# The second layer of a fused attention and feed-forward kernel, transposed and split twice

## The chip, the cores and the metric

The kernel runs on one core of a Trainium2 chip. The metric is device time in microseconds for one execution, from the first to the last instruction with what the device adds around it. Three runs of the kernel before took 933.7, 934.85 and 936.31 us; the median is 934.85. A profile of one more execution shows what each engine did: TensorE multiplies matrices (PE, with its weight loads as PEld), VectorE (DVE), ScalarE (ACT) and GpSimd (POOL) work elementwise, and SyncE (SP) issues DMAs.

## The reference

Four batches of 768 tokens pass through attention with 8 heads of 64 columns, where a query sees only the keys that fall into the same of 16 clusters. The result `x`, 3072 tokens by 512, goes through two matrix products:

```python
def _moe_ref(x, w_in, w_out):            # x 3072x512, w_in 512x2048, w_out 2048x512
    h = x @ w_in
    g = h * (1.0 / (1.0 + np.exp(-1.702 * h)))
    return (g @ w_out).astype(np.float32)
```

Inputs and output are 32-bit floats, except that the weights arrive as 64-bit and are rounded in the kernel.

## The kernel before

Everything is written in the order in which each engine is to run it; no scheduler moves instructions. An engine runs its own list in order, and waits where an operand of another engine isn't there yet or a buffer isn't free. All loads and stores stand in one list, that of SP.

**Attention** takes about the first 350 us. A loop over `t` works on pairs of heads; `scores`, `part`, `exps`, `values`, `row_sums_of` and `normalise` make the transposed result X of one pair and one half of the tokens, a tile of 128 x 384. The weights are rounded beside it (`rounding`), a chunk at a time. X of batches 0 to 2 stays in SBUF (pool `xp`); X of batch 3 is stored to a DRAM tile `kept` (L561) and read back after the first layer of batch 0 (L843).

**The first layer** uses a block method: a product of 2 x 2 blocks is made from seven block products in place of eight, with sums of blocks ahead of and after them. For batch `b`, `first7(b, f, X, T)` makes, for `f` in 0 to 7, blocks `f` and `f + 8` of the 16 blocks of `G`, for both halves of the tokens. Each product has two matmuls (L744, weights stationary, 384 columns of X moving). `sums_w` (POOL, L589) makes the sums of w_in two steps ahead, `sums_x` (DVE) those of X for the next batch. `add` (L735) takes results out of PSUM. `gelu` is a tanh on ScalarE (L579) and a product on DVE (L580).

**The second layer** uses the same method once. `second7(b, n, sg)` works on tokens `n*128` to `n*128+127` of both halves, three times a batch. Here the activations in `G` are stationary and 256 columns of w_out (or of its sums, `Z`) move: seven products of eight matmuls (L801). `sums_g(n)` makes the sums of G on DVE ahead of each `n`, `sums_z` those of w_out on POOL in batch 0. The results lie with tokens on the partitions, so a store is one plain DMA (L807).

A 32-bit matmul is two instructions in the profile: seven products of eight matmuls, three times, are 336 instructions a batch; the first layer has 8 x 7 x 2 x 2 = 224.

**PSUM.** `ps_b` has six banks that both layers use in turn; a bank is free when the last copy or addition has read it.

The last instruction but for the closing of the program is the store of the last block (L807); a test whether the fast path was valid (`okt`, `bad`) ends the program.

Of the kernel before, what the change touches and what calls it, by code (L numbers as in the profile page):

```python
# [8 lines left out]
FP32 = mybir.dt.float32  # L9
# [4 lines left out]
AF = mybir.ActivationFunctionType  # L14
# [24 lines left out]
def fast(  # L39
# [40 lines left out]
    LIMIT = float(2 ** 20)  # L80
    FAR = float(2 ** 120)
    CODE = float(2 ** 50)
    NX = 6 * HP
    SQ = 32
    assert D == 64 and NC == 16 and H * NC == P and NJ == 6 and DM == H * D

# [422 lines left out]
    def values(u):  # L509
        g, kt = divmod(u, NJ)  # L510
        p, h = split(g)
        if kt == 0:
            o_of[g] = ps_o.tile([P, 2, 512], FP32, name="o")
        A = A_of.pop(u)
        for r in range(2):
            rows = slice(r * D, (r + 1) * D)
            for a in range(2):
                nc.tensor.matmul(out=o_of[g][a * D:(a + 1) * D, r, 0:HALF],  # L518
                                 lhsT=v_in[p][rows, a, kt, :],
                                 rhs=A[rows, a, :],  # L520
                                 start=(kt == 0), stop=(kt == NJ - 1))
        if kt == NJ - 1:
            o = o_of.pop(g)
            O_of[g] = (xp if p < NPAIR - HP else xl).tile(
                [P, HALF], FP32, name="x"), short()
            for r in range(2):
                nc.scalar.copy(O_of[g][r], o[:, r, 0:HALF])
# [13 lines left out]
    def normalise(g):  # L541
# [13 lines left out]
        x, more = O_of.pop(g)  # L555
        nc.vector.tensor_tensor(out=x, in0=x, in1=more, op=ALU.add)  # L556
        nc.vector.tensor_tensor(out=x, in0=x, in1=rec, op=ALU.mult)
        if b < B - 1:
            xT_of[b, h, hp] = x
        else:  # L560
            nc.sync.dma_start(out=kept[h, hp], in_=x)  # L561

    recs = {}
    kept = spill.tile([2, HP, P, HALF], FP32, name="kept")

    def check(g):

# [5 lines left out]
                             scale=-2.0 * LIMIT * LIMIT,  # L573
                             accum_out=row_sums[:, 1, g:g + 1])


    def gelu(g, t, h):

        nc.scalar.activation(out=t, in_=h, func=AF.Tanh, scale=1.702)  # L579
        nc.vector.scalar_tensor_tensor(out=g, in0=t, scalar=1.0, in1=h,  # L580
                                       op0=ALU.add, op1=ALU.mult)

    def out_rows(b, h, n):
        return out[b * S:(b + 1) * S, :].rearrange(
            "(j p) n -> p j n", p=P)[:, h * NH + n, :]

    def sums(engine, todo):
        for o, a, op, b in todo:
            engine.tensor_tensor(out=o, in0=a, in1=b, op=(  # L589
                ALU.add if op == "+" else ALU.subtract))  # L590
# [10 lines left out]
    def sums_w(i):  # L601
# [8 lines left out]
        if i < FB:  # L610
# [1 line left out]
        sums(nc.gpsimd, ((S[2], A22, "-", S[3]), (S[1], S[2], "+", A11),  # L612
                         (S[4], A12, "-", S[2])))

    T_of.update({(i, c): tp.tile([P, HALF], FP32, name=f"T{i}{c}")
                 for i in (2, 3, 4) for c in range(2)})

    def sums_x(b):

        X = {(r, h, c): xT_of.pop((b, h, 2 * r + c))  # L620
             for r in range(2) for h in range(2) for c in range(2)}
        T = {(i, c): T_of[i, c] for i in (2, 3, 4) for c in range(2)}
        for c in range(2):
            T[1, c] = X[0, 1, c]
        for o, a, z in ((3, (1, 1), 1), (1, 1, (0, 0)), (2, (1, 1), 1),
# [32 lines left out]
    for t in range(NT + 2):  # L658
# [28 lines left out]
        while work and PREP[work[0][1]] == prep_near:  # L687
            prep(*work.pop(0))
        if t >= NT - 8 and t < NT:
            XT = next(made)  # L690
        for p, i in work:
            prep(p, i)
        for _ in range(0 if t in (0, 1, 2, NT - 1) else 5 if t == 4 else
# [14 lines left out]

    gp = ctx.enter_context(tc.tile_pool(name="gp", bufs=NF // 4))
    yp = ctx.enter_context(tc.tile_pool(name="yp", bufs=1))
    sp = ctx.enter_context(tc.tile_pool(name="sp", bufs=1))
    th = ctx.enter_context(tc.tile_pool(name="th", bufs=1))
    ps_b = ctx.enter_context(tc.tile_pool(name="ps_b", bufs=6, space=PS))
    G = sp.tile([P, NF, 2, HALF], FP32, name="G")
    Z_of = {i: sp.tile([P, FB, DN], FP32, name=f"Z{i}") for i in (2, 3, 4)}
    S4 = [sp.tile([P, 4, P], FP32, name=f"S{q}") for q in range(2)]
    y2 = sp.tile([P, DM], FP32, name="y2")

    def Bz(row, col, f):

        return w_out[:, row * FB + f, col * DN:(col + 1) * DN]

    def Tz(i, f):
        return Bz(0, 1, f) if i == 1 else Z_of[i][:, f]

    def sums_z(f):
        sums(nc.gpsimd, ((Tz(3, f), Bz(1, 1, f), "-", Bz(0, 1, f)),
                         (Tz(1, f), Bz(0, 1, f), "-", Bz(0, 0, f)),  # L730
                         (Tz(2, f), Bz(1, 1, f), "-", Tz(1, f)),
                         (Tz(4, f), Bz(1, 0, f), "-", Tz(2, f))))

    def add(o, p, a):
        nc.vector.tensor_tensor(out=o, in0=p, in1=a, op=ALU.add)  # L735
# [1 line left out]
    def first7(b, f, X, T):  # L737
# [8 lines left out]
            return ps[:, 0:HALF]  # L746

        def finish(g):
            gelu(g, th.tile([P, HALF], FP32, name="th"), g)

        g1, g2 = G[:, f], G[:, f + FB]
        p = product(A_in(0, 0, f), lambda c: X[0, 0, c])
# [16 lines left out]
        finish(g2[:, 0])  # L769
        finish(g1[:, 0])  # L770

    def A_out(h, m, q, n):

        at = m * FB + 4 * q
        return G[:, at:at + 4, h, n * P:(n + 1) * P]

    def sums_g(n):

        S = {}
        for q in range(2):  # L780
            for i in (1, 2, 4):
                S[i, q] = (gp.tile([P, 4, P], FP32, name="g") if i < 4 else
                           S4[q])
            S[3, q] = A_out(1, 0, q, n)
            sums(nc.vector, (
                (S[1, q], S[3, q], "+", A_out(1, 1, q, n)),
                (S[2, q], S[1, q], "-", A_out(0, 0, q, n)),
                (S[4, q], A_out(0, 1, q, n), "-", S[2, q]),
                (S[3, q], A_out(0, 0, q, n), "-", S[3, q])))
        return S  # L790

    def second7(b, n, sg):

        ys = [yp.tile([P, DM], FP32, name="y"), y2]
        C = {10 * (h + 1) + m + 1: ys[h][:, m * DN:(m + 1) * DN]
             for h in range(2) for m in range(2)}

        def product(a, z):
            ps = ps_b.tile([P, 512], FP32, name="b")
            for f in range(FB):  # L800
                nc.tensor.matmul(out=ps[:, 0:DN], lhsT=a(f // 4)[:, f % 4],  # L801
                                 rhs=z(f), start=(f == 0), stop=(f == FB - 1))
            return ps[:, 0:DN]

        def store(h, m=None):
            cols = slice(0, DM) if m is None else slice(m * DN, (m + 1) * DN)
            nc.sync.dma_start(out=out_rows(b, h, n)[:, cols],  # L807
                              in_=ys[h][:, cols])

        p = product(lambda q: A_out(0, 0, q, n), lambda f: Bz(0, 0, f))  # L810
        nc.scalar.copy(C[11], p)  # L811
        p12 = product(lambda q: A_out(0, 1, q, n), lambda f: Bz(1, 0, f))
        p = product(lambda q: A_out(1, 1, q, n), lambda f: Tz(4, f))
        nc.scalar.copy(C[21], p)
        p = product(lambda q: sg[2, q], lambda f: Tz(2, f))
        add(C[22], p, C[11])
        add(C[11], p12, C[11])
        add(C[21], C[22], C[21])
        p = product(lambda q: sg[1, q], lambda f: Tz(1, f))
        add(C[12], p, C[22])  # L820
        p = product(lambda q: sg[3, q], lambda f: Tz(3, f))
        add(C[22], p, C[12])
        add(C[21], p, C[21])
        store(1)
        store(0, 0)
        p = product(lambda q: sg[4, q], lambda f: Bz(1, 1, f))
        add(C[12], p, C[12])
        store(0, 1)

    okt = const.tile([1, 1], FP32, name="okt")  # L830
    bad = const.tile([1, 1], I32, name="bad")
    for b in range(B):
        for f in range(FB):
            first7(b, f, *XT)
            sums_w(b * FB + f + 2)
            if b == 0:
                sums_z(f)
        if b == 0:
            for h in range(2):
                for hp in range(HP):  # L840
                    x = xT_of[B - 1, h, hp] = xp.tile([P, HALF], FP32,
                                                      name="x")
                    nc.sync.dma_start(out=x, in_=kept[h, hp])  # L843
        for n in range(NH):
            sg = sums_g(n)
            if (b, n) == (B - 1, 0):


                ok = const.tile([P, 4, NW], FP32, name="ok")
                nc.vector.tensor_scalar(out=ok, in0=row_sums, scalar1=LIMIT,  # L850
                                        scalar2=None, op0=ALU.is_le)
                ok1 = const.tile([P, 1], FP32, name="ok1")
                nc.vector.tensor_reduce(out=ok1, in_=ok, axis=AX.XY, op=ALU.min)
            if (b, n) == (B - 1, 1):
                ps = bank()
                nc.tensor.transpose(out=ps[0:1, 0:P], in_=ok1, identity=ident)
                nc.vector.tensor_reduce(out=okt, in_=ps[0:1, 0:P], axis=AX.X,
                                        op=ALU.min)
                nc.vector.tensor_scalar(out=bad, in0=okt, scalar1=-1.0,
                                        scalar2=1.0, op0=ALU.mult, op1=ALU.add)  # L860
            if (b, n) == (B - 1, NH - 1):
                is_bad = nc.values_load(bad[0:1, 0:1], min_val=0, max_val=1)
            second7(b, n, sg)
            if n == 1 and b < B - 1:
                *_, XT = sums_x(b + 1)
    return is_bad
@with_exitstack
def general(
# [436 lines left out]
```

## Time and profile before

| | |
|---|---|
| median of three runs | 934.85 us |
| the profiled execution: its time, its span | 936.74 us, 934.8 us |
| first matmul of the first layer | 349.92 us into the span |
| a first layer, a second layer (each of four) | 72.2 to 72.4 us, 72.5 us |
| busy share of PE, DVE, POOL, ACT | 98%, 67%, 45%, 35% |
| matmuls of the second layer: form, time of one as recorded | 128 x 256, 379 ns |
| DMA | 46.65 MB; 127,256 of 138,215 packets under 512 bytes |
| HBM written | 8.05 MB |

In a row of groups stand line, engine, operation, names out<-in, shapes, count, then busy time in us and mean ns of one, then idle time before them and what ended most of it. Matmuls are pipelined, so the recorded 379 ns is longer than the distance from one to the next; the distance is the length of a piece of the chain over its count. A row of the chain has start, length, engine and line. SP's issues are shown with the time from the first to the last of a row.

### The profile page before, as it was taken

The page shows a single profiled execution, that of the slowest core. Times are in us where ns is not written, and L with a number is a line of the kernel's source. Part 1 is how long each engine was busy: PE and PEld are TensorE (multiplying, and loading weights), DVE is VectorE, ACT ScalarE, POOL GpSimd, SP SyncE. Part 2 cuts the span into 40 slices and gives each one's busy share as a digit, 9 for nine tenths or more (in the row PEclk, how much of TensorE's full clock was granted, in tenths as well). Part 3 has the DMA queues.
Part 4 walks back from the last instruction along what each step waited for, and adds up shares of the span by engine and source line. Part 5 has one row for each costly group of instructions (what it writes and reads, how often), then busy time and mean ns, then how long its engine had stood idle before and what let it go on. Part 6 is the DMA issues. An engine that isn't in the chain of part 4 may idle for free.

```text
span 934.8 us, 16594 instructions
## 1 busy us (share of the span) xinstructions
PE 918.1 (98%) x6469; PEld 578.4 (62%) x6469; DVE 623.5 (67%) x1077; ACT 325.5 (35%) x703; POOL 418.5 (45%) x440
## 2 busy tenths in 40 slices
PE   6999999999999999999999999999999999999997
PEld 2344444444444445558886558886557887556886
DVE  3999999989999987775345675354776353677331
ACT  3677767766776762220001231001222000232000
POOL 5799899989998998762001230001321001230000
PEclk8999999999999999999999999999999999999999
DMA  9365546566544300011000000000000000000000
GB/s 182 97 126 110 100 99 132 110 117 122 106 99 99 104 27 10 1 37 31 23 23 22 1 0 1 23 23 24 0 1 1 23 23 23 1 0 1 23 24 26
DMA packets 138215, 46.65 MB, mean 50 GB/s; under 512 B 127256, under 2 KB 132496, under 8 KB 138128
## 3 DMA queue, kind: packets, MB, share of 16 engines
q1 hardware_dynamic: 137984, 45.48, 22.4%
q8 instruction: 53, 0.87, 0.4%
q14 instruction: 34, 0.28, 0.1%
q10 hardware_dynamic: 144, 0.03, 0.0%
HBM read 37.44 MB, written 8.05 MB: 49 GB/s over the span
## 4 chain that ended last, share of the span: by engine, by line
PE 90%; DVE 4%; ACT 2%; issue 1%; DMA 1%; SPq 1%; POOL 0%; ACTq 0%; DVEq 0%
PE b L801 31%; PE b L744 31%; PE s L453 12%; PE o L518 9%; PE s L476 3%; PE m L535 2%; ACT A L484 1%; PE m L329 1%; DMA line<-row 0%; DVE x L556 0%; SPq L404 0%; DMA raw<-in_moe_w_out_dram 0%; DVE e L200 0%; PE m L315 0%; DVE m L193 0%
## 5 line engine op out<-in xcount | busy, mean ns | idle before, releaser
L502 POOL TENSOR_TENSOR sum<-sum,A 128x384 f32<-128x384 f32 x252 | 264.0, 1083 | 39.0 <-ACT A L484 24.8
L589 POOL TENSOR_TENSOR W<-w_in 128x256 f32<-128x256 f32 x32 | 23.4, 730 | 373.3 <-PE b L744 373.1
L484 ACT ACTIVATE A<-s 128x768 f32<-128x768 f32 x192 | 144.6, 804 | 97.2 <-PE s L476 76.5
L735 DVE TENSOR_TENSOR G<-b,G 128x384 f32<-128x384 f32 x224 | 124.3, 555 | 62.8 <-PE b L744 50.4
L453 PE MATMUL s<-T,T 64*64 64x384 f32 x1536 | 145.8, 494 | 2.4 <-ACT A L484 0.6
L735 DVE TENSOR_TENSOR y<-b,y 128x256 f32<-128x256 f32 x72 | 29.4, 422 | 171.8 <-PE b L801 121.9
L518 PE MATMUL o<-A,inv 64*64 64x384 f32 x1536 | 142.5, 486 | 0.0
L579 ACT ACTIVATE th<-G 128x384 f32<-128x384 f32 x128 | 67.0, 523 | 208.2 <-DVE G L735 128.4
L580 DVE SCALAR_TENSOR_TENSOR G<-th,G 128x384 f32<-128x384 f32 x128 | 90.8, 709 | 23.0 <-ACT th L579 19.1
L453 PEld LDWEIGHTS s<-T,T 64*64 64x64 f32 x1536 | 52.8, 132 | 78.9 <-ACT A L484 51.4
L744 PE MATMUL b<-x,W 128*128 128x384 f32 x256 | 93.0, 486 | 0.0
L744 PE MATMUL b<-T,w_in 128*128 128x384 f32 x256 | 93.0, 486 | 0.0
L744 PE MATMUL b<-x,w_in 128*128 128x384 f32 x256 | 88.5, 486 | 0.0
L801 PE MATMUL b<-Z,G 128*128 128x256 f32 x384 | 86.8, 379 | 0.0
L801 PE MATMUL b<-w_out,G 128*128 128x256 f32 x384 | 84.8, 379 | 0.0
L518 PEld LDWEIGHTS o<-A,inv 64*64 64x64 f32 x1536 | 59.7, 134 | 38.5 <-issue 33.4
L801 PEld LDWEIGHTS b<-w_out,G 128*128 128x128 f32 x384 | 72.8, 190 | 10.9
L801 PEld LDWEIGHTS b<-Z,G 128*128 128x128 f32 x384 | 73.0, 190 | 9.9
L744 PEld LDWEIGHTS b<-x,W 128*128 128x128 f32 x256 | 48.6, 190 | 33.9
L744 PEld LDWEIGHTS b<-T,w_in 128*128 128x128 f32 x256 | 48.6, 190 | 33.9
L744 PEld LDWEIGHTS b<-x,w_in 128*128 128x128 f32 x256 | 48.6, 190 | 33.6 <-issue 0.6
L811 ACT COPY y<-b 128x256 f32<-128x256 f32 x12 | 4.5, 372 | 142.0 <-PE b L801 124.5
(120 smaller groups left out, 1126.7 us busy)
## 6 DMA issues: line engine op xcount, KB each, us to landing
raw<-in_moe_w_in_dram SPq DMA_DIRECT2D x16, 512.0 KB
raw<-in_moe_w_out_dram SPq DMA_DIRECT2D x16, 512.0 KB
inv<-in_v_dram SPq DMA_DIRECT2D x16, 384.0 KB
in<-in_q_dram SPq DMA_DIRECT2D x60, 96.0 KB
in<-in_k_dram SPq DMA_DIRECT2D x60, 96.0 KB
out_dram<-y SPq DMA_DIRECT2D x12, 256.0 KB
out_dram<-y SPq DMA_DIRECT2D x24, 128.0 KB
rows<-line SPq DMA_DIRECT2D x120, 1.5 KB
```

What stands on the lines that cost most here:

```text
L453: nc.tensor.matmul(out=ps[c:c + D, a, 0:HALF], lhsT=T[p, 1][rows, kt * P + c:kt * P + c + D], rhs=T[p, 0][rows, h * HALF:(h + 1) * HALF], ...
L476: nc.tensor.matmul(out=s_of[u][c:c + D, a, :], lhsT=rows_of[1, p % 2][rows, kt * P + c:kt * P + c + D], rhs=rows_of[0, p % 2][rows, h * HA ...
L484: nc.scalar.activation(out=A_of[u], in_=s_of.pop(u), func=AF.Exp, scale=SCALE)
L502: nc.gpsimd.tensor_tensor(out=sum_of[g][:, a], in0=(A_of[u - 1] if kt == 1 else sum_of[g])[:, a], in1=A_of[u][:, a], op=ALU.add)
L518: nc.tensor.matmul(out=o_of[g][a * D:(a + 1) * D, r, 0:HALF], lhsT=v_in[p][rows, a, kt, :], rhs=A[rows, a, :], start=(kt == 0), stop=(kt = ...
L535: nc.tensor.matmul(out=ps[a * D:(a + 1) * D, 0:HALF], lhsT=twos, rhs=sm[:, a, :], start=(i == 0), stop=(i == len(parts) - 1))
L579: nc.scalar.activation(out=t, in_=h, func=AF.Tanh, scale=1.702)
L580: nc.vector.scalar_tensor_tensor(out=g, in0=t, scalar=1.0, in1=h, op0=ALU.add, op1=ALU.mult)
L589: engine.tensor_tensor(out=o, in0=a, in1=b, op=(ALU.add if op == "+" else ALU.subtract))
L735: nc.vector.tensor_tensor(out=o, in0=p, in1=a, op=ALU.add)
L744: nc.tensor.matmul(out=ps[:, 0:HALF], lhsT=a[:, c], rhs=x(c), start=(c == 0), stop=(c == 1))
L801: nc.tensor.matmul(out=ps[:, 0:DN], lhsT=a(f // 4)[:, f % 4], rhs=z(f), start=(f == 0), stop=(f == FB - 1))
```

## The change

The second layer is computed transposed: 128 x 128 blocks of w_out are stationary, 192 columns of G move, and the result has output columns on the partitions. The block method is applied twice. The outer seven products are taken one after another, as rounds `k` = 0 to 6 in the order `ORDER`; each round (`second49`) is made of seven inner products of four matmuls, so 49 products where a plain product of 4 x 4 blocks has 64.

- **Sums of the weights.** `sums_z` makes the outer sums in batch 0, now on DVE and POOL. `turn_w` writes one inner sum in place (DVE), and `keep_w` makes the other three on POOL, 21 tiles of 128 x 512, through scratch in `Y`, and stores them to a DRAM tile `kept_w`. `load_sums(k)` reads the three tiles of a round back, two rounds ahead.
- **Sums of G.** The outer ones are made in place (`after7` in the first layer, `sums_G` in rounds 1, 3 and 4), the inner ones by `sums_t(k + 1)` during round `k`, in tiles lent from X's sums, from `Y` and from `E`. All are on DVE.
- **Results.** Inside a round, products are accumulated in PSUM; ScalarE copies and DVE additions make `y`. POOL adds `y` into the four output blocks `Y` (ten sums of 128 x 768 a batch). `store` turns a block in 32 x 32 pieces on DVE and writes it with four DMAs in pieces of 128 bytes. Most stores of a batch are made during the next batch's first layer (`pend`); those of batch 3 in its last round.
- **X.** X of batches 1, 2 and 3 goes to `kept` and is read back a batch ahead; `NX` falls from 24 to 8 buffers.
- **Gelu** is one ScalarE instruction, `Gelu_apprx_sigmoid` with scale 2.

```diff
-        if b < B - 1:
+        if b == 0:
             xT_of[b, h, hp] = x
         else:
-            nc.sync.dma_start(out=kept[h, hp], in_=x)
+            nc.sync.dma_start(out=kept[b - 1, h, hp], in_=x)
...
-    def gelu(g, t, h):
-        nc.scalar.activation(out=t, in_=h, func=AF.Tanh, scale=1.702)
-        nc.vector.scalar_tensor_tensor(out=g, in0=t, scalar=1.0, in1=h,
-                                       op0=ALU.add, op1=ALU.mult)
...
+    FQ = FB // 2
+    QT = HALF // 2
...
+    ws = ctx.enter_context(tc.tile_pool(name="ws", bufs=2))
+    ep = ctx.enter_context(tc.tile_pool(name="ep", bufs=2))
...
+    ORDER = (1, 7, 3, 2, 6, 5, 4)
...
+    def turn_w(i):
+        a = W_of(i)
+        sums(nc.vector, ((a(0, 1), a(0, 0), "-", a(0, 1)),))
+
+    def keep_w(k):
+        a = W_of(ORDER[k])
+        s2, s1, s4 = (Y[n].rearrange("p a t -> p (a t)")[
+            :, 0:FQ * P].rearrange("p (f n) -> p f n", n=P)
+            for n in (12, 21, 22))
+        for i, (o, x, op, z) in enumerate((
+                (s2, a(1, 1), "-", a(0, 1)), (s1, s2, "+", a(0, 0)),
+                (s4, a(1, 0), "-", s2))):
+            sums(nc.gpsimd, ((o, x, op, z),))
+            nc.sync.dma_start(out=kept_w[k, i], in_=o)
+
+    def load_sums(k):
+        W[k] = ws.tile([P, 3, FQ, P], FP32, name="Wz")
+        for i in range(3):
+            nc.sync.dma_start(out=W[k][:, i], in_=kept_w[k, i])
...
+    def sums_t(k, fs=slice(0, FQ)):
+        b = G_of(ORDER[k])
+        t = {i: x[:, fs] for i, x in temps(k).items()}
+        b = {(r, q): b(r, q)[:, fs] for r in range(2) for q in range(2)}
+        for o, x, op, z in ((3, (1, 1), "-", (0, 1)), (2, 3, "+", (0, 0)),
+                            (1, (1, 1), "-", 2), (4, (1, 0), "-", 2)):
...
+            sums(nc.vector, ((t[o], x, op, z),))
+            yield
+
+    def sums_G(i):
+        for f in range(0, FB, 2):
...
+            yield
...
         def finish(g):
-            gelu(g, th.tile([P, HALF], FP32, name="th"), g)
+            nc.scalar.activation(out=g, in_=g, func=AF.Gelu_apprx_sigmoid,
+                                 scale=2.0)
...
+    def after7(f):
+        sums(nc.vector, ((G[:, f, 1], G[:, f + FB, 1], "-", G[:, f, 1]),))
+        if f >= FQ:
+            for _ in sums_t(0, slice(f - FQ, f - FQ + 1)):
+                pass
+
+    def second49(k, extra):
...
+        def product(ps, n, start):
+            for f in range(FQ):
+                nc.tensor.matmul(out=ps, lhsT=A[n][:, f], rhs=M[n][:, f],
+                                 start=start and f == 0,
+                                 stop=(f == FQ - 1), skip_group_check=True)
...
+        product(x, 1, True)
+        nc.scalar.copy(y11, x)
+        z = bank_b()
+        product(z, 2, True)
+        add(y11, z, y11)
+        extra(0)
+        product(x, 6, False)
+        nc.scalar.copy(y12, x)
+        v = bank_b()
+        product(v, 5, True)
+        nc.scalar.copy(p5, v)
+        product(x, 7, False)
+        nc.scalar.copy(y22, x)
+        add(y22, y22, p5)
+        extra(1)
+        product(v, 3, False)
+        add(y12, v, y12)
...
+        product(x, 4, False)
...
+        nc.scalar.copy(y21, x)
+        extra(2)
+        pool = nc.gpsimd
+        sums(pool, {1: (), 7: ((Y[21], y, "+", Y[22]),),
...
+                    5: ((Y[12], y, "+", Y[12]), (Y[22], y, "+", Y[21]))}[i])
...
+    def store(b, n, m, q=slice(0, 2)):
...
+        nc.vector.transpose(out=o, in_=Y[n][:, m, cols])
...
+        for r in range(0, P, SQ):
+            at = (2 * h + m) * P + r
+            nc.sync.dma_start(
+                out=rows[:, at:at + SQ].rearrange("(j t) i -> t j i", t=SQ),
+                in_=o[r:r + SQ].rearrange("t (j i) -> t j i", i=SQ))
...
             first7(b, f, *XT)
             sums_w(b * FB + f + 2)
-            if b == 0:
-                sums_z(f)
+            if f:
+                after7(f - 1)
+            do(pend, 1)
+            if b == 0 and f < 3:
+                for n in range(3 * f, min(3 * f + 3, FB)):
+                    sums_z((nc.gpsimd, nc.vector, nc.vector)[n % 3], n)
+            if b == 0 and f in (3, 4):
+                for i in ORDER[0:4] if f == 3 else ORDER[4:]:
+                    turn_w(i)
+            if b == 0 and f >= 3:
+                for k in {3: (0,), 4: (1, 2), 5: (3,), 6: (4, 5),
+                          7: (6,)}[f]:
+                    keep_w(k)
+        after7(FB - 1)
         if b == 0:
+            load_sums(0)
+            load_sums(1)
...
+        for k in range(7):
+            nxt = sums_t(k + 1) if k < 6 else iter(())
+            more = {1: sums_G(6), 3: sums_G(5), 4: sums_G(4),
+                    5: mixed(stores(b, 11), x_steps),
+                    6: chain(x_steps, stores(b, 12, 22), tail()) if final else
+                    x_steps}.get(k, iter(()))
...
+            def extra(at):
+                do(nxt, (2, 1, 1)[at])
+                do(more, ((3, 1, 1) if final else (3, 3, 3))[at] if k == 6
+                   else (0, 3, 3)[at] if k == 5 else (0, 2, 2)[at])
+
+            second49(k, extra)
+            if k < 5:
+                load_sums(k + 2)
+            elif b < B - 1:
+                load_sums(k - 5)
+        pend = () if final else stores(b, 12, 22, 21)
+        if final:
+            store(b, 21, 1, slice(0, 1))
```

## The prediction

> **What bounds the kernel now.** I read the page's busy times first, then the chain of waits, because a busy engine need not be the one that sets the end.
>
> ```profile
> PE 918.1 (98%) x6469; PEld 578.4 (62%) x6469; DVE 623.5 (67%) x1077; ACT 325.5 (35%) x703; POOL 418.5 (45%) x440
> ```
>
> The chain from the first layer on (start, length, what) is TensorE and nothing else until the last addition:
>
> ```profile
> 349.92 72.44 PE b L744 x224
> 422.36 72.52 PE b L801 x336
> ...
> 880.92 48.36 PE b L801 x224
> 929.28 0.02 issue
> 929.30 0.42 DVE y L735
> ```
>
> Each batch is a first layer (L744, 224 instructions, 72.2 to 72.4 us) and a second one (L801, 336, 72.5 us), with no gap: 323 ns per instruction at 384 moving columns, 215.8 at 256. That is 0.833 ns a column and 2.5 ns fixed. The chain stays on TensorE throughout, so a TensorE instruction saved here is time saved, until another engine comes late. How late they may be is read from busy times by stage (batch 0, first layer, then second; columns PE, PEld, DVE, ACT, POOL, clock, DMA):
>
> ```profile
> 349.92:422.36 72.44, 72.44 (x225) 42.76 (x226) 53.44 (x90) 19.45 (x42) 55.25 (x66) 1.00 0.06 20
> 422.36:494.87 72.51, 72.51 (x337) 63.82 (x337) 30.03 (x56) 3.28 (x8) 4.10 (x4) 1.00 0.08 26
> ```
>
> In the second layer DVE works 30 us of 72.5 and POOL hardly at all. Prices, from the groups:
>
> ```profile
> L801 PEld LDWEIGHTS b<-Z,G 128*128 128x128 f32 x384 | 73.0, 190 | 9.9
> L735 DVE TENSOR_TENSOR y<-b,y 128x256 f32<-128x256 f32 x72 | 29.4, 422 | 171.8 <-PE b L801 121.9
> L589 DVE TENSOR_TENSOR g<-G 128x512 f32<-128x512 f32 x24 | 16.9, 705 | 0.0
> L502 POOL TENSOR_TENSOR sum<-sum,A 128x384 f32<-128x384 f32 x252 | 264.0, 1083 | 39.0 <-ACT A L484 24.8
> L589 POOL TENSOR_TENSOR W<-w_in 128x256 f32<-128x256 f32 x32 | 23.4, 730 | 373.3 <-PE b L744 373.1
> ```
>
> The danger is the first: a weight load is shown with 190 ns, and the change makes matmuls shorter than that. Whether 190 is occupation or latency is seen where the chain of matmuls starts afresh:
>
> ```profile
> 349.85 0.30 PEld L744 LDWEIGHTS b<-x,w_in 128*128 128x128 f32 x2 [0.60 <-issue]
> 349.85 0.59 PE L744 MATMUL b<-x,w_in 128*128 128x384 f32 x1
> ```
>
> Two loads of 190 ns span 0.30 us, so the second began 0.11 after the first, and the first matmul took 0.59 where one in the stream takes 0.486: it began 0.10 after its load did.
>
> [...] the 0.11 and 0.10 above agree, so a load is no bound for a matmul of 160 ns. [...] thin work from 12.5, then half clock until 22.5 (a row ends with clock, DMA share, GB/s).
>
> ```profile
> 12.50:15.70 3.20, 0.94 (x18) 0.75 (x16) 3.13 (x6) 0.80 (x1) 0.95 (x2) 1.00 1.08 236
> 17.00:22.50 5.50, 5.46 (x32) 1.73 (x36) 0.96 (x1) 2.21 (x3) 1.20 (x2) 0.50 1.18 214
> ```
>
> [...] the DVE sum that meets a POOL sum takes 1.21 us, its like without one 0.68.
>
> ```profile
> 424.50 1.06 POOL L589 TENSOR_TENSOR Z<-w_out 128x256 f32<-128x256 f32 x1
> 424.90 1.21 DVE L589 TENSOR_TENSOR g<-G 128x512 f32<-128x512 f32 x1
> ...
> 428.49 0.68 DVE L589 TENSOR_TENSOR g<-G 128x512 f32<-128x512 f32 x1
> ```
>
> **The change, part by part**, against the profiled execution's 936.74 us (span 934.8).
>
> TensorE. A second layer becomes 49 products of 4 matmuls of 2 instructions, 392 of 192 columns: 160 + 2.5 = 162.5 ns, 63.7 us for 72.5. Four batches: **-35.3**.
>
> Gelu. One ScalarE instruction replaces tanh and the DVE product (L580, 128 x 709 ns). One table load is added, 1.28 us as at the start of this trace. Both lie under the first layer (ACT 19 of 72 us): 0. Without that cover the load would cost its 1.28 once. DVE's first-layer work falls: adds 56 x 0.555 = 31, per-f subtractions 8 x 0.55, sums for the first products 16 x 0.35, six transposes of about 0.58 (L545's row), 45 us against 53. Batch 0 has no transposes but sums of w_out (20 x 0.42 and 7 x 0.7), 54 of 72.
>
> Attention. Batches 1 and 2 now store X as batch 3 did (L561); SP waits there for DVE, with the next loads behind it. Batch 3's pairs took 20.6 us like batch 1's 20.5: 0, at most 16 x 0.1 if they show at all.
>
> Batch 0's weight sums. POOL makes 21 sums of 512 columns from round f = 3 on, SP stores each, and only behind the last stands the load of the first ones. POOL at 512: from 0.73 at 256, growing 0.26 (shortest L502) to 0.35 (its mean) per 128: 1.25 to 1.43, I take 1.35. The sums for W of round f+2 are released 2.6 us before round f ends (9.05 each), at 42.65 for f = 4. From there POOL is not idle: f = 4, 4 x 0.73 + 6 x 1.35 = 11.0; f = 5, 2.9 + 4.05 = 7.0; f = 6 (3 W sums now), 2.2 + 8.1 = 10.3; f = 7, 2.2 + 4.05 = 6.25: 77.2, and about 1 for exclusions with DVE: 78.2. Then a store's and a load's issue, 0.33 each, and a landing (the chain shows DMA waits of 1.37 to 3.44 us; 2.1): 81.0. The third product needs it at 72.4 + 2 x 1.3 = 75.0. Stall **+6.0**; the last stored scratch tile is also the target of the first product's copy, which comes to the same time. Idle that long should drop the clock; the early case ran 5.5 us at half, half of it lost: **+2.7**. Bounds: 2 without the clock (POOL at 1.25, landing 1.4, no exclusions: near 3), 13 at 1.43 with longer landings.
>
> Starts of batches 1 to 3. After the last product DVE has an add, two subtractions and 4 + 2 sums of 0.35 before the third product's fourth operand: 3.8 us; needed at 3.6: **+0.6** for three.
>
> Rounds of the second layer. DVE's sums are 768 columns, 0.96 by the 512 and 384 rows (0.69, 0.55). A batch has 24 (one set made earlier leaves 23.0 us), 12 in G 11.5, 8 of X 4.4, 7 small 2.4, 14 adds from PSUM 0.36 each 5.0, two transposes 1.2: 47.5, and 4.3 left over at the start. POOL adds 10 sums of 768, 1.8 each (2.1 by the mean): 18. If every POOL sum shuts DVE out, DVE needs 69.8 of 63.7 us, 6 late; if none does, it is never late. Inside the rounds little is lost, since each round's sums stand a round ahead. The end suffers: in round 5 two POOL sums meet the last sums of X, which the next first layer needs 0.65 to 3.2 us in. Laid out in program order the sixth ends 1.6 late: **+4.8** for three (0 to 18).
>
> Loads per round: three 256 KB, issued when round k's sixth product is through and needed 1.4 rounds later, 13 us for some 3: 0. If that cover went, 28 rounds would pay 1 to 2 us each.
>
> Stores. 49,152 pieces of 128 bytes; this kernel's small-piece traffic averaged 0.224 x 934.8 x 16 / 137,984 = 24 ns apiece, 74 us of DMA time over some 540: hidden. Not so at the end. Each store is four issues for one; 768 pieces cost 0.9 each, a plain one 0.33:
>
> ```profile
> 62.98 3.58 SPq L134 DMA_DIRECT2D in<-in_k_dram  x4
> 929.75 0.33 SPq L807 DMA_DIRECT2D out_dram<-y  x1
> ```
>
> I take 0.40 for 384. In the last round SP starts at about 3.7 us (POOL's sums, then a transpose) and has five stores of 1.6 and two halves of 1.4: 14.5, where TensorE ends at 9.1. So 5.4 behind TensorE, 0.8 now: **+4.6** (3.1 at 0.33, 7 at 0.52).
>
> Sum: -35.3 + 6.0 + 2.7 + 0.6 + 4.8 + 4.6 = -16.6, so 920.1 for the profiled execution, which stands 1.9 above the median shown: **918 us**.
>
> **Rivals.** (a) The covers hold: POOL's stall near 3 and no clock drop, no late sums of X, tail 4: 936.7 - 35.3 + 3 + 0.6 + 4 = 909, median 907. For it: DVE's gelu product, which met POOL most, is gone. Against: the counted 77 us of POOL. (b) Slower: POOL and DVE exclusion becomes the second layer's clock. It decides when a second layer takes over 69.0 us: then 4 x 5.3 and the other 13.9 (6.0, 2.7, 0.6, 4.6) undo the gain. At full exclusion, 69.8, and batch 0 as taken: 936.7 - 35.3 + 13.3 + 24.4 + 0.6 = 939.7, median 938. For it: 1.21 against 0.68. Against: POOL's sums come in ones and twos, and DVE waits for TensorE anyway part of each round. (c) Loads occupy their 190 ns after all: 1568 x 27.5 ns = 43 more, 961; against it stand the 0.11 and 0.10. (d) Loads or SP come late in every round, 28 x 0.5 on top of the forecast: 932, about as before.
>
> **From the cases to the numbers.** Forecast 60% (its own range 911 to 927), (a) 21%, (b) 8%, (c) 3%, (d) 8%. Low 904 takes in (a), high 936 takes in (d) and half of (b). Measurement tells 0.3%, 2.8 us. Faster: all of the forecast and (a), a third of (d), 84%; same 5%; slower 11%.
>
> **What would show it.** L-lines of the second layer at 162.5 ns spacing (190 would be (c)); one gap of about 6 us at the third product of batch 0, released by the weight-sum load or the copy, with half clock after it; POOL's last sum of 512 some 5 us after that first layer ended; second-layer stages of 64 to 66 us in batches 1 to 3, with the wait at the next first layer's second product on a DVE sum of X; SP issuing until about 5 us after the last matmul. It is wrong if stages are near 69 (DVE), or if the attention pairs of batches 1 and 2 leave 20.6.

## The result, and the profile after

The changed kernel takes 925.0 us (median of 4 runs, 924.1 to 925.17); the kernel before took 935.58 beside it (4 runs). The ratio is 0.9887 with an interval of 0.9869 to 0.9906: 10.6 us faster. The forecast was 918, with a range of 904 to 936. The profiled execution has a span of 923.0 us against 934.8, so it accounts for 11.8 us.

The busy line of the page:

```profile
PE 885.7 (96%) x6693; PEld 578.3 (63%) x6693; DVE 714.5 (77%) x1165; ACT 363.4 (39%) x816; POOL 485.0 (53%) x469
```

TensorE is busy 32.4 us less, nearly what the change promised. The span has fallen by a third of that, so TensorE must now wait somewhere. The chain of waits of the changed kernel, from the end of the first layer of batch 0 on, says where (start, length, what):

```profile
425.61 2.61 POOL Y L579 x2
428.60 2.91 DMA Wz<-kept_w
431.65 63.14 PE b L872 x376
494.79 72.24 PE b L822 x224
567.03 63.96 PE b L872 x392
630.99 72.24 PE b L822 x224
703.23 63.96 PE b L872 x392
767.19 72.24 PE b L822 x224
...
903.77 1.87 DMA out_dram<-Tx
...
905.77 0.38 DVE Tx L929
```

Two things are new in it. In batch 0 the chain leaves TensorE for POOL and a load. At its end it passes through SP's issues to the landing of a store (903.77) and the last transpose behind it, which is done at 906.15, while the span goes on to 923.0 with stores alone. Between them, batches 1 to 3 run in equal stages, with no wait of TensorE for a DMA. Busy time by stage shows the same (second layers of batches 0, 1 and 3; columns PE, PEld, DVE, ACT, POOL, clock, DMA):

```profile
421.21:494.79 73.58, 66.21 (x394) 65.61 (x393) 58.93 (x77) 12.80 (x38) 22.64 (x14) 0.95 0.37 120
567.03:630.99 63.96, 63.96 (x393) 63.67 (x393) 54.07 (x74) 11.36 (x35) 15.89 (x7) 1.00 0.25 74
...
839.43:903.40 63.97, 63.97 (x393) 63.41 (x392) 53.02 (x81) 11.37 (x35) 15.57 (x7) 1.00 0.24 70
```

Batch 0 takes 9.6 us longer than the others, with a mean clock of 0.95. The account of the profiled executions, each term a difference of stages:

| term | us | how |
|---|---|---|
| attention up to the first layer | -0.95 | 348.97 against 349.92 |
| four second layers, batch 0 taken like the others | -34.2 | 4 x (63.96 - 72.52) |
| more in batch 0's second layer | +9.6 | 73.58 - 63.96 |
| behind the last product | +14.1 | 923.0 - 903.40 = 19.6; before 934.8 - 929.28 = 5.5 |
| first layers and gaps | -0.3 | 288.96 against 289.16, and a gap of 0.12 that is gone |
| sum | -11.8 | |

The first term isn't a finding. The code of the attention is the same in several of the runs below, and yet the first layer starts at 347.9 to 349.9 us in their profiles. A difference of 1 us between two profiles can be that alone; the stages that follow are counted from their own starts, and so are free of it.

**The stall in batch 0.** The waits between 421 and 436 us in the changed kernel (engine and line, for whom: us in total, times, longest):

```profile
PEld b L872 <- ACT Y L882: 7.6, 1, 7.6
...
PE b L872 <- DMA Wz<-kept_w: 7.3, 1, 7.3
ACT Y L882 <- DMA kept_w<-Y: 6.7, 1, 6.7
```

TensorE waits at the third product for two things at once: the load of the weights' inner sums, and a copy of ScalarE that in turn waits for the store of POOL's last scratch tile. After it TensorE runs at half clock, from 431.65 to 435.3 us, with about 1.8 us lost.

**The tail.** SP's list and its issues in the last stretch (start, time from first to last; then shortest, median and longest in ns):

```profile
896.33 22.10 SPq L933 DMA_DIRECT2D out_dram<-Tx  x36
```
```profile
L933 SPq DMA_DIRECT2D out_dram<-Tx x36: 319/471/1353, 896.3 to 918.0; - x36
```

The 36 issues end at 918.43; the span ends 4.6 later. TensorE's last matmul is recorded until 903.50, 0.1 past the end of its last stage, and from there the issues run on for 14.9 us, the span for 19.5. Below, what lies behind TensorE is counted from the end of that record.

### The profile page after: what moved, and what is told of

Read it like the earlier page. It is cut to its first block, busy times and chain, and to the rows that moved or that the text cites. A ratio compares the mean times of both kernels' runs of the same rounds, so it can differ in the third digit from the quotient of the medians.

```text
span 923.0 us, 17802 instructions
## 1 busy us (share of the span) xinstructions
PE 885.7 (96%) x6693; PEld 578.3 (63%) x6693; DVE 714.5 (77%) x1165; ACT 363.4 (39%) x816; POOL 485.0 (53%) x469
## 4 chain that ended last, share of the span: by engine, by line
PE 77%; DVE 6%; POOL 4%; DMA 3%; issue 3%; SPq 2%; ACT 2%; ACTq 0%; DVEq 0%; POOLq 0%
PE b L822 27%; PE b L872 24%; PE s L453 11%; PE o L518 8%; POOL Y L579 3%; PE m L535 2%; PE s L476 2%; ACT A L484 1%; DMA raw<-in_moe_w_out_dram 1%; DVE G L579 1%; SPq L404 1%; PE m L329 1%; DMA raw<-in_moe_w_in_dram 1%; POOL W L579 1%; DMA line<-row 1%
## 5 line engine op out<-in xcount | busy, mean ns | idle before, releaser
L579 POOL TENSOR_TENSOR Y<-y,Y 128x768 f32<-128x768 f32 x28 | 63.2, 2267 | 207.5 <-DVE y L813 183.5
L827 ACT ACTIVATE G<-G 128x384 f32<-128x384 f32 x128 | 66.3, 523 | 198.4 <-DVE G L813 197.0
L579 DVE TENSOR_TENSOR G<-G 128x768 f32<-128x768 f32 (+1 forms) x88 | 95.8, 1111 | 0.0
L822 PE MATMUL b<-Tx,w_in 128*128 128x384 f32 x256 | 93.0, 486 | 0.0
L822 PEld LDWEIGHTS b<-Tx,w_in 128*128 128x128 f32 x256 | 48.6, 190 | 33.9
L872 PE MATMUL b<-E,Wz 128*128 128x192 f32 x256 | 47.5, 336 | 7.3 <-DMA Wz<-kept_w 7.3
L872 PE MATMUL b<-G,w_out 128*128 128x192 f32 x288 | 50.3, 326 | 0.0
L872 PEld LDWEIGHTS b<-E,Wz 128*128 128x128 f32 x256 | 43.8, 197 | 8.5 <-ACT Y L882 7.6
L872 PEld LDWEIGHTS b<-G,w_out 128*128 128x128 f32 x288 | 47.4, 190 | 1.5 <-ACT G L827 0.3
L822 PE MATMUL b<-Tx,W 128*128 128x384 f32 x128 | 46.5, 486 | 0.0
```

Of the source, the lines that this page charges most:

```text
L579: engine.tensor_tensor(out=o, in0=a, in1=b, op=(ALU.add if op == "+" else ALU.subtract))
L822: nc.tensor.matmul(out=ps[:, 0:HALF], lhsT=a[:, c], rhs=x(c), start=(c == 0), stop=(c == 1))
L827: nc.scalar.activation(out=g, in_=g, func=AF.Gelu_apprx_sigmoid, scale=2.0)
L872: nc.tensor.matmul(out=ps, lhsT=A[n][:, f], rhs=M[n][:, f], start=start and f == 0, stop=(f == FQ - 1), skip_group_check=True)
```

## The experiments

Each was timed beside the kernel before on the same chip, whose median lay between 935.7 and 936.1 us. Ratios are to that kernel; the changed kernel's is 0.9887.

### Two parts of the change alone: gelu, and X kept in DRAM

```diff
# gelu alone, in the kernel before
-            gelu(g, th.tile([P, HALF], FP32, name="th"), g)
+            nc.scalar.activation(out=g, in_=g, func=AF.Gelu_apprx_sigmoid,
+                                 scale=2.0)
# X alone, in the kernel before
-    NX = 6 * HP
+    NX = 2 * HP
...
-            nc.sync.dma_start(out=kept[h, hp], in_=x)
+            nc.sync.dma_start(out=kept[b - 1, h, hp], in_=x)
```

> The kernel before with the activation in one ScalarE instruction instead of the pair of ScalarE and VectorE (one part of the change alone). Prediction's reading: neither engine bounds the first layer, no change, within 0.3% of before (933 to 938 us). Rival (the activation stands in the way of the products' banks): 2 to 4 us faster.

> The kernel before, with the X of batches 1 and 2 kept in DRAM as well (one part of the change alone). Prediction's reading: the stores and loads are covered, no change against the kernel before, within 0.3% (933 to 938 us). Rival (the stores stand in front of the attention's loads on SP's queue, or the loads of X come late at a batch's start): 2 to 5 us slower.

Gelu alone: 935.91 us, ratio 1.0002 (0.9993 to 1.0011). X alone: 935.62, ratio 0.9999 (0.999 to 1.0007). Alone, in the kernel before, both parts cost and bring nothing, as forecast; what moved the time is the new second layer. Whether it could do without them wasn't run. For gelu it is doubtful: VectorE is busy for 65.26 of the 72.24 us of batch 0's first layer in the changed kernel, and the 32 products a batch that gelu no longer asks of it took 0.55 to 0.71 us each before (shortest and mean), so with them it would have 83 to 88 us of work there, an estimate.

### Batch 0: the load, the copy, both

```diff
# direct: the sums of rounds 0 and 1 are made where they are read
+        if k < 2:
+            W[k] = ws.tile([P, 3, FQ, P], FP32, name="Wz")
+            s2, s1, s4 = (W[k][:, j] for j in range(3))
...
-        if b == 0:
-            load_sums(0)
-            load_sums(1)
# scratch: the last scratch tile is not Y[22]
+        if k == 6:
+            s4 = ep.tile([P, 2, HALF], FP32, name="y")...
```

> In batch 0 the weights' inner sums of rounds 0 and 1 are made straight in the tiles that the products read, so that they are not loaded; the first store of POOL's last kept sum from Y[22] stays. Theory (two waits end together: the load for 7.3 us, and the copy into Y[22] for 6.7 us): TensorE still stops, now only behind the copy, and the gain over the changed kernel is 0.5 to 1 us (924 to 924.5 us). Rival (the load alone is the cause, the copy only waits beside it): the stall goes with its half clock, 7.5 + 1.8 us, to about 915.7 us.

> Only the scratch of POOL's last kept sum is moved from Y[22] to another tile, so the copy of the first product does not wait for a store. Loads as they were. Theory (two waits end together): the third product still waits for its weights until about 431.6 us, no change against the changed kernel (925 us, within 0.5). Rival (the copy alone is the cause): the stall goes, about 915.7 us.

> Both edits: no load of the first two rounds' sums in batch 0, and no store behind Y[22]. Theory: a third wait takes over, because VectorE's small sums of X for the third product are shut out by POOL's 512-wide sums until about 429.5 us in the changed kernel; the stall shrinks by 2 us or so and the gain is 2 to 4 us (921 to 923 us). Rival (no third wait): the whole stall and its half clock go, 9.3 us, to 915.7 us.

| edit | us | ratio, interval | TensorE's wait at the third product |
|---|---|---|---|
| no load (direct) | 923.76 | 0.9876, 0.9859 to 0.9892 | 6.4, behind the copy |
| no store behind Y[22] (scratch) | 925.22 | 0.9896, 0.9879 to 0.9912 | 7.0, behind the load |
| both | 922.78 | 0.9866, 0.9849 to 0.9882 | 3.9 in two parts, behind VectorE |

The times of the first two lie within the intervals of the changed kernel's; it is the waits in their traces that tell them apart. Each single edit leaves the stall to the other wait, and both together to a third. With both edits TensorE's wait in the same stretch is:

```profile
PE b L879 <- DVE E L579: 3.9, 2, 3.2
```

VectorE's small sums for the third product are what is late now (sums of G, not of X as the expectation has it). The theory held in all three, with the first 0.2 us below its range, and the rivals, by which the whole stall would have gone, fall. What holds up VectorE was still argued here; the next run tests it.

### Batch 0: POOL's sums begun earlier

```diff
# with both edits
-            if b == 0 and f in (3, 4):
-                for i in ORDER[0:4] if f == 3 else ORDER[4:]:
+            if b == 0 and f in (2, 3):
+                for i in ORDER[0:4] if f == 2 else ORDER[4:]:
                     turn_w(i)
-            if b == 0 and f >= 3:
-                for k in {3: (0,), 4: (1, 2), 5: (3,), 6: (4, 5),
+            if b == 0 and f >= 2:
+                for k in {2: (0,), 3: (1,), 4: (2, 3), 5: (4,), 6: (5,),
                           7: (6,)}[f]:
                     keep_w(k)
```

> No load of the first two rounds' sums in batch 0, no store behind Y[22], and the weights' sums of POOL begun one feature block earlier, in POOL's idle time before 387 us, so that its last one ends 3 to 5 us earlier. Theory (with the load and the copy away, TensorE waits for VectorE's small sums, and these for POOL's last 512-wide sums): the stall of 4.7 us that is left with both edits alone falls to 0 to 1.5 us and its half clock goes: 917 to 919.5 us. Rival (VectorE is late for another reason): as with both edits alone, 922.8 us.

It took 918.38 us, ratio 0.9815 (0.9799 to 0.9832), 6.6 us faster than the changed kernel. POOL's last sum now starts at 423.94 and ends at 425.3 us, and VectorE's sums go at full speed from there on. The timeline (start, length; idle before in brackets):

```profile
423.94 1.38 POOL L579 TENSOR_TENSOR y<-w_out,Y 128x512 f32<-128x512 f32 x1
424.22 1.30 DVE L579 TENSOR_TENSOR E<-Y,G 128x192 f32<-128x192 f32 x1
...
426.95 0.36 DVE L579 TENSOR_TENSOR E<-Y,G 128x192 f32<-128x192 f32 x1
```

The same sum takes 1.30 us beside POOL and 0.36 without it. The wait of TensorE falls to 2.1 us, more than the 0 to 1.5 expected; the half clock is gone in this trace (1.00 throughout), and the second layer of batch 0 takes 66.3 us from its first matmul to that of the next layer; it took 73.4 in the changed kernel, 72.6 without the load and 71.0 with both edits. About 1.1 us came back in the first layer of batch 0, 73.4 for 72.3, which now has the weights' work earlier. So POOL's late end was the cause of the third wait. That the other two hang on it as well is seen in the changed kernel's trace, where POOL's last sum ends at 428.2 and its store and the load follow at once; the earlier sums alone, with the load and the copy left as they were, were not run.

### The ends of the second layers: POOL against VectorE

The forecast had 4.8 us for late sums of X at the ends of the second layers; the trace shows none. Do POOL's sums hold up VectorE's, and how near is that to TensorE? The first run gives POOL one sum more, the second gives all of POOL's second-layer sums to VectorE.

```diff
# one more
+        if i == 5 and more_pool[0]:
+            sums(pool, ((y, y, "+", Y[12]),))
...
# all on VectorE
-        pool = nc.gpsimd
+        pool = nc.vector
```

> One POOL sum of 768 columns more in round 5 of batches 0 to 2 (its result is not used). Theory (VectorE and POOL exclude each other, and the next batch's sums of X are done only 0.4 us before they are needed): VectorE is 1.8 to 2.3 us later at the end of each of three second layers, TensorE waits 1.4 to 1.9 us each time, the time rises by 4 to 6 us to 929 to 931 us. Rival (the exclusion is harmless, VectorE has room): no change, 925 us within 1.

> The seven 768-column sums a batch that POOL makes in the second layer are made by VectorE instead; nothing else differs from the changed kernel. Theory (the two exclude each other, so that POOL's help costs VectorE about as much as it saves: the seven took 15.9 us on POOL in batch 1 and held up VectorE's sums for some 9 us, while VectorE makes seven in 6.1 us): VectorE is not later, no change or 0 to 1.5 us faster, 923.5 to 925 us. Rival (POOL relieves VectorE): 6.1 us more on VectorE in each second layer, more than the margin of some 1.2 us at the three following first layers, 3 to 10 us slower, 928 to 935 us.

One more on POOL: 926.49 us, ratio 0.9909 (0.9892 to 0.9925), 1.5 slower than the changed kernel where 4 to 6 were expected. The extra sum took 2.0 us and did hold VectorE up. The timeline of VectorE at the end of batch 1, first in the changed kernel (next layer from 630.99), then in this one (from 631.87):

```profile
630.19 1.01 DVE L579 TENSOR_TENSOR Tx<-x 128x384 f32<-128x384 f32 x2
```
```profile
631.06 2.36 DVE L579 TENSOR_TENSOR Tx<-x 128x384 f32<-128x384 f32 x2
```

These two sums ended 0.2 us into the next layer, and end 1.55 into it now. The layers that follow take 72.35 to 72.42 us for 72.24, so TensorE has only just begun to wait: the margin was about 1.2 us, not the 0.4 of the expectation. Of the 1.5 us by which its span is longer, 0.5 is in these stages, and that alone can be put down to the edit; 0.9 stands ahead of the first layer of batch 0, where the edit changes nothing.

All on VectorE: 922.09 us, ratio 0.9854 (0.9837 to 0.987). The rival's 3 to 10 us slower is out, and it is faster by 2.9, more than the 1.5 allowed. The group of VectorE's sums of G in the second layer of batch 1, in the changed kernel and with POOL idle:

```profile
L579 DVE TENSOR_TENSOR G<-G 128x768 f32<-128x768 f32 x14 | 19.3, 1411 | 0.0
```
```profile
L579 DVE TENSOR_TENSOR G<-G 128x768 f32<-128x768 f32 x14 | 12.8, 950 | 0.0
L579 DVE TENSOR_TENSOR Y<-y,Y 128x768 f32<-128x768 f32 x7 | 6.5, 950 | 0.2 <-ACT y L907 0.2
```

The seven sums cost VectorE 6.5 us of its own, and these 14 alone got 6.5 shorter. The help of POOL was worth nothing here: a sum of G took 1411 ns on average with POOL at work and 950 with it idle. By what POOL's sums hold up VectorE's is not shown. The gain itself is in the tail: in the last round the two sums ahead of the stores take 1.79 us where POOL took 4.14, SP starts 8.9 us ahead of TensorE's end where it started 7.2 ahead, and ends 11.8 behind it for 14.9; the span ends 16.5 us behind TensorE for 19.5.

### The tail: where are the stores issued from, and in what pieces?

```diff
# a third of the last round's stores from ScalarE's queue
-            nc.sync.dma_start(
+            (nc.scalar if b == B - 1 and (n, m) in (
+                (22, 0), (22, 1), (21, 0)) else nc.sync).dma_start(
...
-                do(more, ((3, 1, 1) if final else (3, 3, 3))[at] if k == 6
+                do(more, ((2, 2, 1) if final else (3, 3, 3))[at] if k == 6
```

> In the last round of the last batch 12 of the 36 stores are issued from ScalarE's queue and one more of the output's blocks is done a place earlier or later so that both queues have work. Theory (the tail is bound by SP's issuing, 36 issues of about 0.52 us and a few of over 1): SP has 24 issues left, the end comes 6 to 10 us earlier, 915 to 919 us. Rival (VectorE's last sums or the transfers bind the tail): 0 to 1 us, 924 to 925 us.

921.15 us, ratio 0.984 (0.9824 to 0.9856): 3.9 us faster, between the two. SP has fewer issues, but they don't go faster (0.75 us from one to the next, where it was 0.61), and now some wait for earlier transfers. Both queues in the timeline, and SP's waits from 895 us on:

```profile
897.00 18.02 SPq L934 DMA_DIRECT2D out_dram<-Tx  x24
902.85 11.15 ACTq L934 DMA_DIRECT2D out_dram<-Tx  x12
```
```profile
SPq L934 <- DMA out_dram<-Tx: 3.3, 5, 1.1
```

In the changed kernel SP waits for no transfer in this stretch. The share of the DMA engines between 903 and 907 us is 0.79, where the changed kernel has 0.54. So SP's issuing did bind, but close behind it stand the transfers of 128-byte pieces. The second queue brought 3.9 us of the 7.4 that 12 issues fewer should have brought (12 x 22.10 / 36, an estimate). What should help against both is larger pieces:

```diff
# the blocks (22) and (21) of the last batch
+    def turn_out(b, n, m, o, copy, queue):
+        ps = ps_b.tile([P, 512], FP32, name="b")[:, 0:HALF]
+        for j in range(HALF // P):
+            nc.tensor.transpose(out=ps[:, j * P:(j + 1) * P],
+                                in_=Y[n][:, m, j * P:(j + 1) * P],
+                                identity=ident)
+        copy(o, ps)
+        queue.dma_start(                       # 384 pieces of 512 bytes
...
-            store(b, 21, 1, slice(0, 1))
+            turn_out(b, 22, 0, T_of[4][:, 0], act, nc.scalar)
+            turn_out(b, 22, 1, T_of[4][:, 1], dve, nc.scalar)
+            turn_out(b, 21, 0, Y[11][:, 0], act, nc.sync)
+            turn_out(b, 21, 1, Y[11][:, 1], dve, nc.sync)
```

> In the last batch the blocks (22) and (21) are turned by TensorE in pieces of 128 columns (12 transposes behind its last product) and stored in 4 transfers of 384 pieces of 512 B, two on ScalarE's queue, instead of by VectorE in 20 transfers of 128-B pieces. Theory (the tail is bound by the number of issues and of small pieces, on whichever queue): SP has 16 small stores left until about 905 us and 2 of the 4 large ones, TensorE ends about 1.5 us later, and the end comes 10 to 14 us earlier than in the changed kernel, 911 to 915 us. Rival (the tail is bound by the last sums of VectorE and POOL, or by a fixed latency behind the last product): 0 to 3 us, 922 to 925 us.

917.06 us, ratio 0.9803 (0.9787 to 0.982): 7.9 us faster, short of the expected 10, but the rival's 0 to 3 is out. The span ends 9.2 us behind TensorE instead of 19.5. What ends last is one order of work (timeline; idle before and what ended it in brackets):

```profile
903.66 2.16 ACTq L949 DMA_DIRECT2D out_dram<-Tx  x2
...
905.86 0.48 ACT L946 COPY Y<-b 128x384 f32<-128x384 f32 x1 [2.23 <-DMA out_dram<-Tx]
907.18 1.34 SPq L949 DMA_DIRECT2D out_dram<-Y  x2
```

The view puts the third copy down to a landing; but it stands behind two issues in ScalarE's own list, the second of which took 1.64 us and ended at 905.82, just ahead of it. The last stores stand behind this copy.

### The pieces together

The run with the earlier sums was given the same tail, with block (12) turned by TensorE too, all copies ahead of the issues and all stores on SP; then, in a second one, also VectorE for POOL's sums.

```diff
-            turn_out(b, 22, 1, T_of[4][:, 1], dve, nc.scalar)
+            parts = [turn_out(b, 22, 0, T_of[4][:, 0], act),
+                     turn_out(b, 22, 1, T_of[4][:, 1], dve),
...
# in the second one
-        pool = nc.gpsimd
+        pool = nc.vector
```

> Weights' sums begun earlier as in the run before, and block (12) also turned by TensorE, so that the last round has 8 small stores and 6 of 512-B pieces, all on SP's queue, and no copy waits behind an issue on ScalarE's queue. Theory (the tail goes with the issues and the small pieces): what lies behind the last product falls from 19.6 us to 6 to 8 us, against the run with the earlier sums alone (918.4 us) a gain of 11 to 13 us, 905 to 908 us. Rival (the gain ends where it ended with 16 small stores, about 9.2 us behind the last transposes, since the landing of the last stores sets it): 908 to 911 us.

> The fastest kernel so far (weights' sums early, last blocks turned by TensorE, 910.8 us) with the same seven sums on VectorE. Theory: as above, and since the sums of blocks (12) and (22) are ready earlier in the last round, 0 to 1.5 us faster, 909 to 911 us. Rival: 3 to 10 us slower, 914 to 921 us.

The first took 910.79 us, ratio 0.9733 (0.9715 to 0.975), the second 909.66, ratio 0.9723 (0.9707 to 0.9739): the fastest here, 15.3 us under the changed kernel. The second is as expected, but their intervals overlap. The first of the two is a miss: it gained 7.6 us on the earlier sums alone, where 11 to 13 were expected, and lies where the rival put it. What lies behind TensorE did fall from 19.5 us to 8.3. That is only 0.9 less than the 9.2 of the run with 16 small stores, so the order of the copies, eight small stores fewer and the single queue came to no more than that together. Its last stores in the timeline:

```profile
892.34 4.19 SPq L940 DMA_DIRECT2D out_dram<-Tx  x8
899.10 2.87 SPq L957 DMA_DIRECT2D out_dram<-Tx  x4
902.07 1.74 SPq L957 DMA_DIRECT2D out_dram<-Y  x2
```

The last issue ends at 903.8, only 2.3 us behind TensorE, but 6.0 remain to the end of the span. Also, 18 transposes take TensorE 2.0 us, of which the first 0.7 stand ahead of the last product. Against the profile with the earlier sums alone, the first layer began 1.3 us later, and the second layer of batch 0 took 1.7 us longer, though nothing was changed there. The second of these is the clock, which stands at half for one stretch (columns as in the rows by stage):

```profile
428.86:432.27 3.41, 3.41 (x11) 3.41 (x12) 2.59 (x5) 0.32 (x1) 0.00 (x0) 0.50 0.92 268
```

With the earlier sums alone TensorE waited 0.85 and 1.20 us at this place, and the clock did not drop. The 370 instructions behind the waits took 60.39 us there and in the second of the two runs here, and 62.07 in this one; why the clock dropped is not shown. The margin of the earlier sums is thin: the same code there cost nothing more, or 1.7 us.

## Why the prediction was right, and where it was not

- **TensorE, -35.3.** Right: -34.2. 392 instructions in 63.96 us, of which 0.26 is the wait at the start of the layer, are 162.5 ns each. Rival (c) is out, though weight loads recorded at 190 ns fill 63.67 us of the 63.96.
- **Gelu, attention, X, loads, 0.** Right: 1.0002 and 0.9999 for the first and third alone, and no wait for a load in rounds of batches 1 to 3. Rival (d) is out.
- **The stall of batch 0, +6.0, and the clock, +2.7.** Right in place and cause: POOL's last sum of 512 ended 7.0 us after the first layer where 5.8 was counted; the wait was 7.3, the clock cost 1.8. The step named the copy as a second wait that ends at the same time; the runs showed that there is a third, VectorE's sums behind POOL's.
- **The starts of batches 1 to 3, +0.6.** Each second layer begins 0.26 us late, 0.8 for three: about right.
- **The ends of the second layers, +4.8.** Wrong: 0. The step that failed is VectorE's price. Its sums of 768, priced at 0.96, follow each other at 0.87, since the next begins before the record of the last has ended. In batch 1 VectorE has no idle time from 601.48 us to the end of the sixth sum of X at 631.20: its 35 instructions are recorded at 32.2 us in all and take 29.7. If the forecast laid its prices end to end, as its sum of 47.5 does, that is 2.5 of the 2.8 us between "the sixth ends 1.6 late" and the margin of 1.2 found above, an estimate. The two POOL sums did meet the last sums of X as forecast, two of which took 2.17 and 1.67 us instead of 0.55. "POOL adds 10 sums of 768, 1.8 each" is a miscount (so is the ten in the account of the change): in the trace of the changed kernel there are 28, seven a batch, of 2.27 us. What the ten did to the forecast beyond the 69.8 of full exclusion (an estimate of its own; full exclusion was not shown) stays open. POOL's sums do hold up VectorE's, as rival (b) said (1411 ns against 950), but stages of 63.96 put rival (b) out.
- **The tail, +4.6.** Wrong in size: +14.1, the largest miss. The step counted "five stores of 1.6 and two halves of 1.4", which is 28 issues; there are 36, since VectorE came to block (11), which stands in round 5, only at 895.73, 1.5 us into the last round, so that its eight stores fell there as well. And "I take 0.40 for 384" was 0.47 with 0.05 between two, and over 1 us for three of the 36; with a wait of 0.95 the mean is 0.61. The case given as an end, 7 us at 0.52, had the price of an issue nearly right and the count wrong.

Rival (a) was right about the sums of X alone: the stall was 7.3 with a drop of the clock, where it had near 3 and none, and the tail 14.1 for 4.

The two misses oppose each other, which is luck: 4.8 too much at the ends, 9.5 too little in the tail. With 0.9 more in batch 0's second layer (9.6 for 8.7), 0.5 more in the second layers at large (-34.2 for -35.3 and +0.6) and 1.25 less in the attention and the first layers, they make the 4.8 by which -16.6 missed -11.8. The forecast was right about the sign and the bulk. Its time was 7 us low: these 4.8, and 1.9 that it took off since the profile before stood that much above its median, while the profile after (924.83) stands at its own.

## What to carry to other kernels

A saving on the engine that sets the pace is worth what it says only up to the next wait, and a wait may have several that end together: take them all away before you call one of them not the cause. Price a row of instructions by the distance from one to the next, not by their records. Count what stands in a queue at the end of the kernel, in number of issues and in pieces; nothing hides it there: with four stores in 512-byte pieces for 20 in 128-byte pieces the time fell by 7.9 us, while small pieces cost nothing in the middle of this kernel (batches 1 to 3 in equal stages, with no wait of TensorE for a DMA). Work given to GpSimd beside VectorE's sums was no relief here: seven sums moved to it spared VectorE 6.5 us, and 14 of its own took 6.5 us longer.

## What the runs showed of the hardware

- The records of sums on VectorE overlap: two sums of 768 columns, recorded at 0.95 us each, are together recorded at 1.82 in the changed kernel (from 602.62 us on; 1.79 with all sums on VectorE), and the next instruction begins 1.74 us after the first did.
- A store issue on SP takes 0.47 us at 384 pieces and 0.44 at 192, medians of the changed kernel's last round: half the pieces took 0.03 off. Single issues there are longer: three of 1.11 to 1.35 us in the changed kernel, up to 1.39 on SP and 1.61 on ScalarE with two queues, 1.64 on ScalarE with the turned blocks; why is not shown.
- From the end of the last issue to the end of the span it is 4.7 us in the kernel before, 4.6 in the changed one and with POOL's sums on VectorE, 4.7 with two queues, 4.8 with the turned blocks, and 5.1 and 6.0 in the two fastest; why is not shown.
- A recorded weight load of 190 ns is no bound at a spacing of 162.5, in the second layers of batches 1 to 3.
- TensorE's clock was at half for 6.8 us from 428.5 us on in the changed kernel, 4.2 us into a wait of 7.3. It was at half for 3.4 us from 428.86 us on in one of three traces with the same code at that place; in one of the other two the waits there were 0.85 and 1.20 us.
